# Linear attention into four experts: chunk loads ahead of w2, scaling ahead of the state update, late first updates, casts tied to stages

## The chip, the core and the metric

The kernel runs on one core of a Trainium2 chip. The core has five engines, each with its own instruction queue that it works off in order: TensorE (PE; its weight loads are shown apart as PEld), VectorE (DVE), ScalarE (ACT), GpSimd (POOL) and SyncE (SP), which here issues nearly all transfers. They wait for one another by semaphores. The metric is the device time of one execution in microseconds, lower is better.

## The reference

Two parts, one after the other, all in fp32:

```python
# attention, per batch b (4) and head h (8), head_dim 48, over t = 0..767
cur   = outer(u * k[t], v[t])
y[t]  = r[t] @ (state + cur)
state = w[:, None] * state + outer(k[t], v[t])
# experts: x is y as 3072 rows x 384; 4 experts, D = 384, F = 1024
p    = domain_probs / (domain_probs.sum(-1) + 1e-9)
out += p[:, e] * (relu(x @ w1[e]) @ w2[e])      # for each e
```

## The kernel before

**Tiling.** The 768 time steps of a batch are cut into 6 chunks of 128. Chunk number `ci` counts over batches first (`b = ci % 4`, `c = ci // 4`), so chunks 0 to 3 are the first 128 steps of all four batches and make one sub-sequence of 512 rows for the experts; there are 6 sub-sequences and 24 chunks. Weights are loaded as fp32 in three pieces per expert and matrix (`load_w1`, `load_w2`) into 8 staging buffers `wst`, and rounded to bf16 by `cast_w1`, `cast_w2` on ScalarE ("A") or VectorE ("V"). A piece can be loaded only when the cast eight pieces earlier has freed its buffer.

**One chunk of attention** goes through these steps. `load` brings r, k, v (192 KB each, four buffers of each). `scale_rk` multiplies r and k by powers of w on VectorE (lines 214, 215) into `RK`, of which there are four. `ruk_vb` multiplies r, k and u on GpSimd and rounds v. `stRK` transposes RK on TensorE (line 246) and copies the result out on ScalarE (254); for chunks 8 and up it is a transposing transfer. `diag` sums r·u·k on VectorE (230) and multiplies it with v on GpSimd (231, `dv`). `stAt` makes the 128 x 128 score blocks on TensorE (261) and masks them on VectorE (267). `stY` multiplies with the old state (278) and with v (285), and VectorE adds dv and rounds (289, `Ysb`). `stX` transposes Ysb (328) and VectorE copies it (329) to `xTe`, the experts' input. `stS` makes the state update on TensorE (306), then VectorE (315 in the first chunk of a batch, else 317) and GpSimd (318).

**Experts.** `l1` makes one 128-wide slice of the hidden layer for 512 rows (three matmuls, line 341; ScalarE's Relu, 345), `l1q` four slices for one chunk (355, 359), `l2` one chunk's output (eight matmuls, 368), weighted on ScalarE for expert 0 (374) and added up on VectorE for the others (376).

**PSUM.** Score blocks, transposes and the pair Y and state update have one buffer each (tags `At`, `tr`, `ys`); the expert outputs share four (`mm`). A step that writes into one of the single buffers waits until the last reader of the step before is done.

**Order.** All queues follow the order in which the program calls the helpers. A hand-written list (lines 389 to 454) holds chunks 0 to 3, with expert 0 of sub-sequence 0 woven in; `spin` puts matmuls of no use between, and only keeps TensorE at work. After it a loop goes over slots, one for each expert and sub-sequence: 12 places per slot, eight `l1` of this expert and four `l2` of the slot before. Attention steps of chunks 4 and up come from `att_steps()`, three for every four places in the first three slots, then one for every two. The table `casts` ties casts and loads to places of the slots; from chunk 4 on `diag` also loads the next chunk not yet loaded, starting with chunk 8.

Of the kernel before, what the change touches and what calls it, by code (L numbers as in the profile page):

```python
# [18 lines left out]
def kernel(  # L19
# [367 lines left out]
    with tc.manual_schedule(engines={ET.PE, ET.Pool, ET.DVE, ET.Activation, ET.SP}):  # L387

        wu_consts()
# [56 lines left out]
        stX(3)
        stS(3)
        for i in range(3):
            cast_w1(1, i, "AVA"[i])
# [3 lines left out]
        l1q(0, 0, 0, 3)
        l1q(0, 0, 4, 3)


        casts = {(0, 1): [lambda: cast_w2(1, 0, "A")], (0, 2): [lambda: cast_w2(1, 1, "V")],
                 (0, 6): [lambda: cast_w2(1, 2, "A"), lambda: (load_w2(2), load(6))],
                 (0, 7): [lambda: cast_w1(2, 0, "A")], (0, 8): [lambda: cast_w1(2, 1, "V")],
                 (0, 10): [lambda: cast_w1(2, 2, "A"), lambda: (load_w1(3), load(7))],  # L460
                 (1, 2): [lambda: cast_w2(2, 0, "A")], (1, 3): [lambda: cast_w2(2, 1, "V")],
                 (1, 5): [lambda: cast_w2(2, 2, "A"), lambda: load_w2(3)],
                 (1, 9): [lambda: cast_w1(3, 0, "A")], (1, 10): [lambda: cast_w1(3, 1, "V")],
                 (1, 11): [lambda: cast_w1(3, 2, "A")],
                 (2, 7): [lambda: cast_w2(3, 0, "A")], (2, 8): [lambda: cast_w2(3, 1, "V")],
                 (2, 9): [lambda: cast_w2(3, 2, "A")]}

        def att_steps():

            for ci in range(SUB, 2 * SUB):  # L470
# [4 lines left out]
                if ci == 2 * SUB - 1:
                    yield lambda: (head(2 * SUB), diag(2 * SUB))
                yield lambda ci=ci: stX(ci)
                yield lambda ci=ci: stS(ci)
# [71 lines left out]
```

## Time and profile before

| | us |
|---|---|
| median of 3 runs (316.89 to 319.53) | 319.11 |
| profiled execution | 318.16 |
| its span, first to last instruction | 316.4 |
| TensorE busy | 294.4 (93%) |
| VectorE, ScalarE, GpSimd busy | 162.7, 154.7, 106.0 |

The mean granted clock of TensorE is 0.987. The busy time of TensorE is its matmuls' own time; how it is spread over the span, and what it waited for where it was idle, is read from stretches and from the timeline. Idle time of another engine matters only where TensorE waits for what that engine makes.

### The profile page before, as it was taken

How to read it: one execution, taken by the hardware profiler on the slowest of the kernel's cores; microseconds unless marked ns; L12 is line 12 of the kernel's file. 1: busy time of each engine (PE TensorE's matmuls, PEld its weight loads, DVE VectorE, ACT ScalarE, POOL GpSimd, SP SyncE). 2: the span in 40 equal slices, each digit the busy share in tenths (PEclk: the TensorE clock that was granted, in tenths of full speed). 3: DMA queues.
4: the chain of work that ended last, by engine and by line, in shares of the span. 5: the costliest groups of instructions: out<-in, count | busy, mean ns of one | idle time of the engine just before them, and what ended most of it. 6: DMA issues, size and time to landing. Idle time of an engine off the chain costs nothing.

```text
span 316.4 us, 5360 instructions
## 1 busy us (share of the span) xinstructions
PE 294.4 (93%) x2048; PEld 161.1 (51%) x2081; DVE 162.7 (51%) x292; ACT 154.7 (49%) x249; POOL 106.0 (34%) x137
## 2 busy tenths in 40 slices
PE   6896987878999999999999999999999999999995
PEld 3355643434545555555555555555555555555552
DVE  5785867574954556754464673475461432201223
ACT  4555696634435644345534446434446344465440
POOL 3543335535642542552462364165441000000000
PEclk9997999997999999999999999999999999999999
DMA  8989999999577626446515645810432000200002
GB/s 188 244 247 299 253 269 277 275 225 229 108 172 170 79 43 123 77 117 147 108 33 102 133 102 121 110 33 16 96 85 46 15 12 0 77 25 0 2 0 99
DMA packets 111053, 37.63 MB, mean 119 GB/s; under 512 B 99226, under 2 KB 111004, under 8 KB 111028
## 3 DMA queue, kind: packets, MB, share of 16 engines
q1 hardware_dynamic: 111012, 37.29, 51.0%
q8 instruction: 16, 0.26, 0.4%
q14 instruction: 9, 0.07, 0.1%
q10 hardware_dynamic: 16, 0.00, 0.0%
HBM read 26.79 MB, written 4.72 MB: 100 GB/s over the span
## 4 chain that ended last, share of the span: by engine, by line
PE 80%; DVE 11%; ACT 3%; POOL 2%; issue 2%; DVEq 0%; POOLq 0%
PE out_ps L368 37%; PE hT_ps L341 34%; DVE AtM L267 3%; PE At_ps L261 2%; DVE RK L215 2%; PE Y_ps L285 2%; DVE RK L214 1%; ACT w_sb L84 1%; DVE oacc L376 1%; DVE Ysb L289 1%; PE spin_ps L164 1%; DVE dcoef L230 1%; PE Y_ps L278 1%; ACT hTs L345 1%; PE hT_ps L355 1%
## 5 line engine op out<-in xcount | busy, mean ns | idle before, releaser
L345 ACT ACTIVATE hTs<-hT_ps 128x512 bf16<-128x512 f32 x184 | 109.8, 598 | 114.6 <-PE hT_ps L341 106.8
L368 PE MATMUL out_ps<-w_sb,hTs 128*128 128x384 bf16 x768 | 141.2, 328 | 0.0
L341 PE MATMUL hT_ps<-xTe,w_sb 128*128 128x512 bf16 x519 | 138.1, 380 | 1.9 <-issue 0.2
L368 PEld LDWEIGHTS <-hTs 128*128 128x128 bf16 x768 | 75.1, 98 | 58.5 <-issue 1.7
L376 DVE SCALAR_TENSOR_TENSOR oacc<-out_ps,p_nat,oacc 128x384 f32<-128x384 f32 x72 | 44.3, 615 | 96.1 <-PE out_ps L368 92.0
L341 PEld LDWEIGHTS <-w_sb 128*128 128x128 bf16 x552 | 50.0, 98 | 46.0
L318 POOL TENSOR_TENSOR S<-Tn,wC 64x192 bf16<-64x192 f32 x32 | 17.1, 534 | 89.3 <-DVE Tn L317 82.3
L267 DVE TENSOR_TENSOR AtM<-At_ps,mask 128x512 bf16<-128x512 f32 x48 | 30.9, 685 | 17.0 <-PE At_ps L261 17.0
L222 POOL TENSOR_TENSOR ruk<-Rt,Kt 128x384 f32<-128x384 f32 x24 | 25.5, 1061 | 12.7 <-DMA Kt<-in_k_dram 11.4
L231 POOL TENSOR_TENSOR dv<-Vt,dcoef 128x384 f32<-128x384 f32 x24 | 20.4, 848 | 27.1 <-DVE dcoef L230 27.1
L223 POOL TENSOR_TENSOR ruk<-ruk,U_sd 128x384 f32<-128x384 f32 x24 | 27.1, 1130 | 2.8 <-ACT U_sd L177 1.0
L215 DVE TENSOR_TENSOR RK<-Kt,W_sd 128x384 bf16<-128x384 f32 x24 | 25.9, 1081 | 0.0
L374 ACT ACTIVATE oacc<-out_ps,p_nat 128x384 f32<-128x384 f32 x24 | 14.0, 583 | 17.6 <-PE out_ps L368 17.6
L230 DVE TENSOR_REDUCE dcoef<-ruk 128x8 f32<-128x384 f32 x24 | 13.1, 544 | 9.9 <-POOL ruk L223 9.8
L84 ACT CAST w_sb<-wst 128x1152 bf16<-128x1152 f32 (+1 forms) x18 | 17.7, 1008 | 0.0
L289 DVE TENSOR_TENSOR Ysb<-Y_ps,dv 128x384 bf16<-128x384 f32 x24 | 13.2, 552 | 8.2 <-PE Y_ps L285 6.8
L214 DVE TENSOR_TENSOR RK<-Rt,W_sd 128x384 bf16<-128x384 f32 x24 | 16.3, 677 | 2.2 <-ACT W_sd L175 2.1
L317 DVE TENSOR_TENSOR Tn<-S,St_ps 64x192 f32<-64x192 bf16 x32 | 11.3, 352 | 11.8 <-PE St_ps L306 10.8
L224 POOL CAST Vb<-Vt 128x384 bf16<-128x384 f32 x24 | 16.3, 681 | 0.0
L285 PE MATMUL Y_ps<-Vb,AtM 128*128 128x48 bf16 x192 | 10.0, 184 | 3.7 <-DVE AtM L267 2.4
L246 PE MATMUL RKT_ps<-ident,RK 128*128 128x128 bf16 x64 | 6.1, 232 | 7.8 <-DVE RK L214 3.6
L254 ACT COPY RKT<-RKT_ps 128x1024 bf16<-128x1024 bf16 x7 | 7.1, 1012 | 9.0 <-PE RKT_ps L246 9.0
(55 smaller groups left out, 113.5 us busy)
## 6 DMA issues: line engine op xcount, KB each, us to landing
wst<-in_moe_w_dram SPq DMA_DIRECT2D x16, 576.0 KB, 6.0
Rt<-in_r_dram SPq DMA_DIRECT2D x24, 192.0 KB, 3.4
Kt<-in_k_dram SPq DMA_DIRECT2D x24, 192.0 KB, 3.7
Vt<-in_v_dram SPq DMA_DIRECT2D x24, 192.0 KB, 5.3
out_dram<-oacc SPq DMA_DIRECT2D x24, 192.0 KB, 2.7
wst<-in_moe_w_dram SPq DMA_DIRECT2D x8, 384.0 KB, 6.8
RKT<-RK SPq DMA_TRANSPOSE x16, 3.2
xTe<-Ysb SPq DMA_TRANSPOSE x16, 2.5
```

The source lines that it names most:

```text
L84: nc.scalar.copy(o, i)
L214: nc.vector.tensor_mul(RK[:, 0, :, 0:D], Rt, W1_sd)
L215: nc.vector.tensor_mul(RK[:, 1, :, 0:D], Kt, W2_sd)
L222: nc.gpsimd.tensor_mul(ruk, s["Rt"], s["Kt"])
L223: nc.gpsimd.tensor_mul(ruk, ruk, U_sd)
L231: nc.gpsimd.tensor_mul(dv, s["Vt"], dcoef.to_broadcast((128, H, D)))
L267: nc.vector.tensor_mul(s["AtM"][:, j], ps[:, j], mask[:, None, :].to_broadcast((128, NP, C)))
L318: nc.gpsimd.tensor_mul(S_new[pr, :, cl], Tn[pr], wCb)
L341: nc.tensor.matmul(ps[:, 0:n, :].rearrange("p a b -> p (a b)"), w1_sb[:, e, db, fb * 128:(fb + 1) * 128], xTe[:, db, s0:s0 + n, :].rearran ...
L345: nc.scalar.activation(hTs[:, fb, s0:s0 + n, :], ps[:, 0:n, :], AF.Relu)
L368: nc.tensor.matmul(ps, hTs[:, fb, s, :], w2_sb[:, e, fb, :], start=(fb == 0), stop=(fb == NFB - 1))
L376: nc.vector.scalar_tensor_tensor(oaccs[ci], in0=ps, scalar=pe, in1=oaccs[ci], op0=ALU.mult, op1=ALU.add)
```

## The change

Six things, in the order of the diff. The spin matmuls read a tile of ones of their own, written first of all on VectorE, and there are 29 instead of 24, three of them at the very start. Chunks 2 and 3 are loaded ahead of expert 0's w2. The bank in which p is transposed is one of the four shared ones. `diag` of chunk 4 loads nothing any more, so chunk 8 is loaded by chunk 5's. In the hand-written list `diag` and `scale_rk` stand earlier, casts of w2 are spread, and the state updates of chunks 0 to 3 move behind it: chunk 0's to its end, the other three into the first slot. In the slots `scale_rk` of the next chunk stands between a chunk's `stY` and `stX`, and casts are keyed by attention step instead of by place.

```diff
+    spin_in = consts.tile([128, 4, 128], BF16)
+    nc.vector.memset(spin_in, 1.0)
...
     load(1)
-    load(2)
     prow = consts.tile([TOTC, C, E], F32)
     nc.sync.dma_start(prow, moe_domain_probs.rearrange("(n p) e -> n p e", p=C))
+    load(2)
+    load(3)
     load_w2(0)
-    load(3)
...
-            nc.tensor.matmul(ps, ident, mask[:, None, :].to_broadcast((128, 4, 128)),
-                             start=True, stop=True)
+            nc.tensor.matmul(ps, spin_in[:, 0, :], spin_in, start=True, stop=True)
...
-        pp = psum.tile([128, E, TOTC], F32, tag="ys", bufs=1, name="p_ps")
+        pp = psum.tile([128, E, TOTC], F32, tag="mm", bufs=4, name="p_ps")
...
-        if ci >= SUB and loaded[0] < TOTC:
+        if ci > SUB and loaded[0] < TOTC:
...
         scale_rk(1)
         ruk_vb(1)
-        stS(0)
         spin(2)
         l1q(0, 0, 0, 0)
         stRK(1)
+        diag(1)
         scale_rk(2)
-        diag(1)
         ruk_vb(2)
         l1q(0, 0, 4, 0)
         spin(2)
         stAt(1)
         stRK(2)
+        diag(2)
         spin(4)
         stY(1)
-        spin(3)
+        load_w1(1)
+        spin(2)
         stX(1)
         stAt(2)
-        stS(1)
-        diag(2)
+        scale_rk(3)
+        ruk_vb(3)
+        load(4)
         l1q(0, 0, 0, 1)
         l1q(0, 0, 4, 1)
-        for i in range(3):
-            cast_w2(0, i, "A")
-        load_w1(1)
-        load_w2(1)
-        load(4)
         stY(2)
-        scale_rk(3)
-        ruk_vb(3)
+        stRK(3)
+        cast_w2(0, 0, "A")
+        diag(3)
         spin(2)
         stX(2)
-        stRK(3)
+        stAt(3)
+        l1q(0, 0, 0, 2)
+        cast_w2(0, 1, "A")
+        load_w2(1)
+        load(5)
         p_consts()
...
+        casts = {("At", 4): [c2(1, 0)], ("Y", 4): [c2(1, 1)],
+                 ("H", 4): [c2(1, 2), lambda: (load_w2(2), load(6))],
+                 ("X", 4): [c1(2, 0)], ("S", 4): [c1(2, 1)],
+                 ("At", 5): [c1(2, 2), lambda: (load_w1(3), load(7))],
+                 ("H", 5): [c2(2, 0)], ("X", 5): [c2(2, 1)],
+                 ("S", 5): [c2(2, 2), lambda: load_w2(3)],
+                 ("At", 6): [c1(3, 0)], ("Y", 6): [c1(3, 1)], ("H", 6): [c1(3, 2)],
+                 ("Y", 7): [c2(3, 0)], ("H", 7): [c2(3, 1)], ("X", 7): [c2(3, 2)]}
...
+            yield lambda: (scale_rk(SUB), ruk_vb(SUB))
             for ci in range(SUB, 2 * SUB):
-                yield lambda ci=ci: (scale_rk(ci), ruk_vb(ci))
-                yield lambda ci=ci: (stRK(ci), diag(ci))
-                yield lambda ci=ci: stAt(ci)
-                yield lambda ci=ci: stY(ci)
...
+                yield step("RK", ci, lambda: stRK(ci), lambda: diag(ci))
+                yield step("At", ci, lambda: stAt(ci))
+                yield step("Y", ci, lambda: stY(ci))
+                if ci + 1 < 2 * SUB:
+                    yield step("H", ci, lambda: scale_rk(ci + 1), lambda: ruk_vb(ci + 1))
+                else:
+                    yield step("H", ci, lambda: head(ci + 1), lambda: diag(ci + 1))
+                yield step("X", ci, lambda: stX(ci))
+                yield step("S", ci, lambda: stS(ci))
...
+        late = {(0, 1): [lambda: stS(1)], (0, 5): [lambda: stS(2)], (0, 9): [lambda: stS(3)]}
```

In the order the change shows itself as follows; each row is an instruction of one engine's queue. First VectorE in the hand-written list, from the masking of chunk 2 on, before (RK_135 and RK_137 are chunk 3's):

```order
L267 TENSOR_TENSOR AtM<-At_ps,mask 128x512 x2
L315 TENSOR_TENSOR S_1_143<-St_ps,wC 64x4x48 x2
L230 TENSOR_REDUCE dcoef<-ruk 128x8
L289 TENSOR_TENSOR Ysb<-Y_ps,dv 128x384
L214 TENSOR_TENSOR RK_135<-Rt,W_sd 128x8x48
L215 TENSOR_TENSOR RK_135<-Kt,W_sd 128x8x48
L329 COPY xTe<-xT_ps 128x3x128
```

and with the change:

```order
L268 TENSOR_TENSOR AtM<-At_ps,mask 128x512 x2
L215 TENSOR_TENSOR RK_137<-Rt,W_sd 128x8x48
L216 TENSOR_TENSOR RK_137<-Kt,W_sd 128x8x48
L290 TENSOR_TENSOR Ysb<-Y_ps,dv 128x384
L231 TENSOR_REDUCE dcoef<-ruk 128x8
L330 COPY xTe<-xT_ps 128x3x128
L268 TENSOR_TENSOR AtM<-At_ps,mask 128x512 x2
```

The scaling of chunk 3 stands ahead of the rounding of chunk 2's Y, and the state update of chunk 1 is gone from between.

Then SyncE's queue around chunk 6, before (the three Rt are of chunks 5, 8 and 6, the three wst the pieces of expert 2's w2):

```order
L107 DMA Rt_600<-in_r_dram 128x8x48
L107 DMA Kt_601<-in_k_dram 128x8x48
L107 DMA Vt_602<-in_v_dram 128x8x48
L107 DMA Rt_696<-in_r_dram 128x8x48
L107 DMA Kt_697<-in_k_dram 128x8x48
L107 DMA Vt_698<-in_v_dram 128x8x48
L79 DMA wst_720<-in_moe_w2_dram 128x3x384
L79 DMA wst_722<-in_moe_w2_dram 128x3x384
L79 DMA wst_724<-in_moe_w2_dram 128x2x384
L107 DMA Rt_726<-in_r_dram 128x8x48
L107 DMA Kt_727<-in_k_dram 128x8x48
L107 DMA Vt_728<-in_v_dram 128x8x48
```

and with the change (pieces of expert 2's w1 and w2, then chunks 6 and 8):

```order
L73 DMA wst_606<-in_moe_w1_dram 128x3x384
L73 DMA wst_608<-in_moe_w1_dram 128x3x384
L73 DMA wst_610<-in_moe_w1_dram 128x3x256
L79 DMA wst_748<-in_moe_w2_dram 128x3x384
L79 DMA wst_750<-in_moe_w2_dram 128x3x384
L79 DMA wst_752<-in_moe_w2_dram 128x2x384
L107 DMA Rt_754<-in_r_dram 128x8x48
L107 DMA Kt_755<-in_k_dram 128x8x48
L107 DMA Vt_756<-in_v_dram 128x8x48
L107 DMA Rt_811<-in_r_dram 128x8x48
L107 DMA Kt_812<-in_k_dram 128x8x48
L107 DMA Vt_813<-in_v_dram 128x8x48
```

Chunk 8 now follows chunk 6, and expert 2's w1 and w2 stand together behind chunk 5.

Last VectorE around the scaling of chunk 7 (RK3), before:

```order
L86 CAST w1_sb_70<-wst_783 128x3x384
L289 TENSOR_TENSOR Ysb_1003<-Y_ps_990,dv_947 128x384
L376 SCALAR_TENSOR_TENSOR oacc_667<-out_ps_1006,p_nat_166,oacc_667 128x384
L329 COPY xTe_762<-xT_ps_1016 128x3x128
L317 TENSOR_TENSOR Tn_1037<-S2_1_145,St_ps_1032 64x192 x2
L376 SCALAR_TENSOR_TENSOR oacc_554<-out_ps_1042,p_nat_166,oacc_554 128x384
L214 TENSOR_TENSOR RK3_135<-Rt_787,W1_sd_162 128x8x48
L215 TENSOR_TENSOR RK3_135<-Kt_788,W2_sd_163 128x8x48
L230 TENSOR_REDUCE dcoef_1075<-ruk_1054 128x8
```

and with the change:

```order
L290 TENSOR_TENSOR Ysb_1006<-Y_ps_993,dv_951 128x384
L86 CAST w1_sb_70<-wst_843 128x3x384
L377 SCALAR_TENSOR_TENSOR oacc_659<-out_ps_1009,p_nat_168,oacc_659 128x384
L215 TENSOR_TENSOR RK3_137<-Rt_847,W1_sd_164 128x8x48
L216 TENSOR_TENSOR RK3_137<-Kt_848,W2_sd_165 128x8x48
L330 COPY xTe_777<-xT_ps_1038 128x3x128
L377 SCALAR_TENSOR_TENSOR oacc_564<-out_ps_1043,p_nat_168,oacc_564 128x384
L318 TENSOR_TENSOR Tn_1058<-S2_1_147,St_ps_1053 64x192 x2
L231 TENSOR_REDUCE dcoef_1079<-ruk_1021 128x8
```

The scaling has moved ahead of the copy of chunk 6's transposed Y, of one multiply-add and of chunk 6's state update.

## Rows read from the trace of the kernel before

**Rows 1.** Stretches: start:end length, busy per engine, PEclk, DMA share, GB/s.

```profile
0.00:38.20 38.20, 30.03 (x277) 18.62 (x279) 25.54 (x60) 19.97 (x29) 15.30 (x26) 0.96 0.94 246
38.20:50.10 11.90, 8.98 (x72) 4.65 (x73) 8.72 (x13) 9.94 (x16) 5.65 (x7) 1.00 0.99 253
50.10:66.10 16.00, 14.09 (x116) 7.41 (x116) 10.63 (x19) 10.09 (x14) 7.58 (x10) 1.00 1.00 267
66.10:83.00 16.90, 14.24 (x96) 7.46 (x97) 10.74 (x20) 7.54 (x11) 9.03 (x12) 0.90 0.87 203
...
88.00:316.40 228.40, 223.25 (x1463) 121.03 (x1489) 102.32 (x176) 105.94 (x178) 64.20 (x80) 1.00 0.35 74
```

**Rows 2.** Timeline, TensorE: start, us, instruction, [idle before, releaser].

```profile
24.78 0.34 PE L328 MATMUL xT_ps<-ident,Ysb 128*128 128x128 bf16 x3 [1.28 <-DVE Ysb L289]
...
26.78 0.61 PE L246 MATMUL RKT_ps<-ident,RK 128*128 128x128 bf16 x8 [1.66 <-DVE xTe L329]
...
38.21 1.24 PE L341 MATMUL hT_ps<-xTe,w_sb 128*128 128x512 bf16 x5
...
49.15 0.40 PE L246 MATMUL RKT_ps<-ident,RK 128*128 128x128 bf16 x4 [1.56 <-DVE RK L214]
```

**Rows 3.** Timeline from w1's cast to the next sub-sequence.

```profile
61.26 1.16 ACT L84 CAST w_sb<-wst 128x1152 bf16<-128x1152 f32 x1
...
65.91 0.62 DVE L376 SCALAR_TENSOR_TENSOR oacc<-out_ps,p_nat,oacc 128x384 f32<-128x384 f32 x1
...
66.44 0.35 DVE L329 COPY xTe<-xT_ps 128x384 bf16<-128x384 bf16 x1
...
69.62 1.16 DVE L214 TENSOR_TENSOR RK<-Rt,W_sd 128x384 bf16<-128x384 f32 x1
...
70.70 1.34 DVE L215 TENSOR_TENSOR RK<-Kt,W_sd 128x384 bf16<-128x384 f32 x1
...
70.84 0.40 PE L246 MATMUL RKT_ps<-ident,RK 128*128 128x128 bf16 x4 [1.14 <-DVE RK L214]
...
72.11 0.40 PE L246 MATMUL RKT_ps<-ident,RK 128*128 128x128 bf16 x4 [0.87 <-DVE RK L215]
...
83.03 0.81 PE L341 MATMUL hT_ps<-xTe,w_sb 128*128 128x512 bf16 x3
```

**Rows 4.** SyncE's transfers: issue time in ns, start, landing; chunks 7, 6, w1.

```profile
L107 SPq DMA_DIRECT2D Rt<-in_r_dram x1: 679/679/679, 56.6 to 56.6; - x1
DMA to landing us min/median/max: 7.3/7.3/7.3
...
L107 SPq DMA_DIRECT2D Kt<-in_k_dram x1: 1032/1032/1032, 50.0 to 50.0; - x1
DMA to landing us min/median/max: 6.3/6.3/6.3
...
L73 SPq DMA_DIRECT2D wst<-in_moe_w_dram x1: 591/591/591, 54.9 to 54.9; - x1
DMA to landing us min/median/max: 5.7/5.7/5.7
```

**Rows 5.** Timeline, VectorE, a scaling without GpSimd beside it.

```profile
78.89 0.55 DVE L214 TENSOR_TENSOR RK<-Rt,W_sd 128x384 bf16<-128x384 f32 x1
...
79.36 0.55 DVE L215 TENSOR_TENSOR RK<-Kt,W_sd 128x384 bf16<-128x384 f32 x1
```

**Rows 6.** Waits of SyncE: us in total, times, longest.

```profile
SPq L107 <- POOL dv L231: 9.4, 6, 3.0
```

**Rows 7.** Chain of waits, one L1 and one L2 group.

```profile
78.31 0.65 PE hT_ps L341 x3
78.96 1.30 PE out_ps L368 x8
```

**Rows 8.** Stretches, the two with a low clock (PEclk behind POOL).

```profile
26.80:30.40 3.60, 3.60 (x36) 3.28 (x35) 1.00 (x4) 1.61 (x2) 0.96 (x2) 0.69 1.02 359
72.30:76.10 3.80, 3.58 (x16) 1.54 (x16) 0.21 (x1) 1.61 (x2) 3.34 (x5) 0.55 1.06 224
```

More of the change, by code (lines that the diff above doesn't have):

```diff
@@ L387 @@
     with tc.manual_schedule(engines={ET.PE, ET.Pool, ET.DVE, ET.Activation, ET.SP}):
+        spin(3)
         wu_consts()
@@ L395 @@
         w_consts()
-        spin(3)
+        spin(1)
         stAt(0)
@@ L399 @@
             cast_w1(0, i, "A")
-        spin(3)
+        spin(4)
         stY(0)
@@ L416 @@
         stRK(2)
+        diag(2)
         spin(4)
         stY(1)
-        spin(3)
+        load_w1(1)
+        spin(2)
         stX(1)
         stAt(2)
-        stS(1)
-        diag(2)
+        scale_rk(3)
+        ruk_vb(3)
+        load(4)
         l1q(0, 0, 0, 1)
         l1q(0, 0, 4, 1)
-        for i in range(3):
-            cast_w2(0, i, "A")
-        load_w1(1)
-        load_w2(1)
-        load(4)
         stY(2)
-        scale_rk(3)
-        ruk_vb(3)
+        stRK(3)
+        cast_w2(0, 0, "A")
@@ L434 @@
+        diag(3)
         spin(2)
         stX(2)
-        stRK(3)
+        stAt(3)
[3 more added lines that the diff above has]
+        load(5)
         p_consts()
-        l1q(0, 0, 0, 2)
         l1q(0, 0, 4, 2)
-        stAt(3)
-        diag(3)
-        stS(2)
+        stY(3)
+        cast_w2(0, 2, "A")
+        spin(3)
+        stX(3)
+        spin(1)
+        cast_w1(1, 0, "A")
+        cast_w1(1, 1, "V")
         l2(0, 0, 0)
-        stY(3)
+        l1q(0, 0, 0, 3)
@@ L445 @@
         l2(0, 0, 1)
[L446 to L449, printed above, removed]
+        l1q(0, 0, 4, 3)
+        cast_w1(1, 2, "A")
         load_w1(2)
-        load(5)
         l2(0, 0, 2)
[L453 to L466, printed above, removed]
+        stS(0)
@@ new lines, in c1, with c2 @@
+        def c1(e, i):
+            return lambda: cast_w1(e, i, "AVA"[i])
+        def c2(e, i):
+            return lambda: cast_w2(e, i, "AVA"[i])
+        casts = {("At", 4): [c2(1, 0)], ("Y", 4): [c2(1, 1)],
[6 more added lines that the diff above has]
+                 ("Y", 7): [c2(3, 0)], ("H", 7): [c2(3, 1)], ("X", 7): [c2(3, 2)]}
@@ L468, in att_steps, with step, do @@
+        def step(name, ci, *fs):
+            def do():
+                for f in fs:
+                    f()
+                for f in casts.get((name, ci), ()):
+                    f()
+            return do
         def att_steps():
+            yield lambda: (scale_rk(SUB), ruk_vb(SUB))
             for ci in range(SUB, 2 * SUB):
-                yield lambda ci=ci: (scale_rk(ci), ruk_vb(ci))
-                yield lambda ci=ci: (stRK(ci), diag(ci))
-                yield lambda ci=ci: stAt(ci)
@@ L474, in att_steps @@
-                yield lambda ci=ci: stY(ci)
[L475 to L478, printed above, removed]
+                yield step("RK", ci, lambda: stRK(ci), lambda: diag(ci))
[5 more added lines that the diff above has]
+                    yield step("H", ci, lambda: head(ci + 1), lambda: diag(ci + 1))
@@ L503 @@
                 for g in range(3):
-                    for f in casts.get((si, 3 * q + g), ()):
+                    for f in late.get((si, 3 * q + g), ()):
                         f()
```

## The prediction

> **What bounds the kernel now.** I read the stretches first, then the waits inside them. After 88 us TensorE is busy 223.25 of 228.40 us [rows 1], so nothing that the change does can come from there; what it does before 88 us is either kept to the end or lost. The first four stretches are the prologue (to 38.2) and the slots of experts 1, 2 and 3 on sub-sequence 0 (to 50.1, 66.1 and 83.0). TensorE idles in them 8.2, 2.9, 1.9 and 2.7 us by subtraction. In the same rows the transfers are the second bound: the DMA share is 0.94 to 1.00 up to 66.1 us, at 246 to 267 GB/s. So before 66 us the work can be made earlier only as far as its bytes have landed.
>
> The waits themselves: TensorE waits for VectorE. In the prologue 1.28 us for Y's rounding of chunk 2 and 1.66 us for the copy that frees the one transpose bank [rows 2]; in the expert-1 slot 1.56 us for the scaling of chunk 5 [rows 2]; at chunk 7 1.14 and 0.87 us for its two scalings [rows 3]. In rows 3 the reader is to see why the last is late: VectorE is done with its multiply-add at 65.91 + 0.62 = 66.53, then come the transposed copy and the state update, and only at 69.62 the scaling of chunk 7, whose r had landed at 56.6 + 7.3 = 63.9 us [rows 4]. The transfer was 5.7 us early, and the order of the program was what held it.
>
> **The change, part by part.**
>
> *Scaling ahead of the state update.* For chunk 7 it now stands right behind the multiply-add, ahead of the copy and of the state update. Two bounds. If nothing upstream moves, it starts at 66.53 and saves 69.62 − 66.53 = 3.1 us. If upstream moves by 2.6 us or more, it waits for r at 63.9 and saves 5.7 us; it can't save more, since chunk 7's transfer stands behind the same bytes as before (chunks 0 to 6 and 8, three pieces each of w1 of experts 0 to 3 and of w2 of experts 0 to 2, in either order). I take the second, 63.95, since the next parts move more than 2.6 us.
>
> What the move costs there: both engines that read r and k are now released by the same landing, so GpSimd multiplies beside the scaling. Alone the two instructions take 0.55 us each [rows 5]; beside GpSimd they took 1.16 and 1.34 us [rows 3]. I take the slow pair: 63.95 + 2.50 = 66.45. The transposed copy of chunk 6 (0.35 us, rows 3) is now behind it on VectorE and frees the transpose bank, so the eight transposes, half of which used to run during the scaling, all start at 66.45 + 0.35 + 0.14 of hand-offs (two gaps of 0.07, as between 70.70 + 1.34 = 72.04, the scaling's end, and the transposes at 72.11) = 66.9 and take 0.61 (the eight of [rows 2]), to 67.5. Before, they ended at 72.11 + 0.40 = 72.5. **Saved: 5.0 us.** [...]
>
> *Does upstream move by 2.6 us?* In the prologue chunk 3 (3 x 192 KB) no longer stands behind w2 of expert 0 (576 + 576 + 384 KB), which at 246 GB/s was 6.4 us of transfer; r, k of chunk 3 are scaled ahead of Y's rounding of chunk 2, so their transposes come in the place of the wait of 1.66 us; dv is ready a stage earlier because diag follows stRK, which takes the wait of 1.28 us. Together 2.9 us, against 38.21 for the first expert-1 matmul [rows 2]. In the expert-1 slot the wait of 1.56 us for chunk 5 goes the same way. That is 4.5 us of named waits, of which 2.6 are needed; the 1.9 over are not a gain, they are cover. Out of this cover I pay what I cost at nothing: the memset of the spin operand, 29 spin matmuls in place of 24, the casts now tied to stages, and w2 of expert 0, which lands one chunk (590 KB / 246 GB/s = 2.4 us) later. If the cover is gone, each us too late costs one us until only 3.1 are saved.
>
> *Loads.* Chunk 8 was loaded in chunk 4's diag, ahead of chunk 6; now chunk 5's diag does it, behind chunk 6. Chunk 6's k had landed at 50.0 + 6.3 = 56.3 [rows 4]; without chunk 8 ahead of it, 2.2 to 2.4 us earlier (590 KB at 267 and 246 GB/s), about 54.0. It is needed when chunk 5's Y has been rounded, some 51 to 52 by the same shift, so VectorE waits there up to 2.5 us: that is where most of the prologue's gain ends, and why I don't count it. The loads by diag waited 9.4 us in all on SyncE for dv of the same chunk [rows 6]; now their buffers are a stage older, so this wait goes, but SyncE's wait cost TensorE nothing.
>
> w1 of expert 3: first piece at 54.9 + 5.7 = 60.6 [rows 4], the same bytes ahead of it as before. Its cast takes 1.16 us [rows 3], so expert 3's slot can start at 61.8 instead of 66.1 [rows 1]. From there to the transposes of chunk 7 at 66.9 it has three L1 groups (0.65 each) and one L2 group (1.30) [rows 7], 3.3 us, and a few small transposes: TensorE waits there about 1.5 us, and this transfer sets nothing.
>
> *The four late state updates* are 16 small matmuls and 8 VectorE instructions, the same as before, in other places; they share one PSUM bank with Y, and I put a wait of 0.5 us each on TensorE for it, all ahead of 50 us and so under the cover.
>
> *Behind chunk 7.* [...] The one behind chunk 7 costs 3.8 x (1 − 0.55) = 1.7 us, and I take it as gone: one wait of about 1.5 us is left there in place of 1.14 and 0.87 with matmuls between. **Saved: 1.7.** [...]
>
> VectorE's backlog at 67 us (copy, multiply-add, state update, reduction: about 2.5 us) makes chunk 7's masking late by about **0.5 us, lost**. From expert 3's slot on the order is as before, TensorE-bound at 98% [rows 1], and the gain is kept.
>
> Sum: 5.0 + 1.7 − 0.5 = 6.2 us off the profiled execution's 318.16 us (span 316.4): **312.0 us**. The median of the three runs is 319.11 and the profiled execution lies 0.95 below it, inside their spread of 316.89 to 319.53; I keep 312.0 and let the range carry the 0.95.
>
> **The rivals.**
>
> *The clock falls once more* at the wait behind chunk 7 or chunk 6. For: two such falls in the trace. Against: single waits, as the 1.56 us in rows 2, left the clock at 1.00 in rows 1. Price 1.7 us: 313.7.
>
> *The wait moves, and the gain with it.* VectorE and ScalarE take their work in order, and the change puts instructions that need a transfer (scaling of chunks 6 and 7, casts of w1 of expert 3) ahead of evictions that need none. If the transfers come 2.6 us or more behind those of before, because SyncE meets a buffer that a later cast frees, chunk 7 is scaled at 66.5 as in the lower bound: 3.1 + 0 − 0.5 = 2.6 saved with the clock's fall kept, 315.6; 4 us behind, 317. For: DMA share 1.00, no slack in the stream. Against: equal bytes ahead, and SyncE's waits were for dv, which now go.
>
> [...]
>
> **How the numbers follow.** Forecast at full clock 0.42, one fall of the clock 0.28, the moved wait 0.20, the long low clock 0.10. A measurement of this kernel can tell about 1% (3.2 us) from no change; the first two cases are beyond that (0.70 faster), the third within it (0.20), the last slower (0.10). Likeliest time 312.0. Range: down to 308.5, if the scaling of chunk 7 takes its lone 1.1 us instead of 2.5 and its transfer comes 1 us sooner, with the 1.2 us by which the lowest run stands under the profiled one; up to 317, which takes in the fall and nearly all of the moved wait. The long low clock and the end of the third case are left out.
>
> **What would show it.** Right: the first scaling of chunk 7 at 64 us, ended by a DMA; its transposes done by 68; expert 3's slot from about 62 and the first matmul of the next sub-sequence (83.03 before, rows 3) at 76 to 77; granted clock 1.00 there; the rest as long as before. Wrong: chunk 7's r later than 65 us, VectorE idle for a transfer over 3 us, or a clock under 0.9 in a slot.

## The result and the profile after

The changed kernel takes 310.12 us (median of 4, 309.42 to 311.79) against 319.32 us (316.89 to 320.03) beside it on the same chip: a ratio of 0.9733, 95% interval [0.9668, 0.9797]. In two later comparisons it took 309.78 us, 0.9767 [0.9724, 0.9809], and 309.95 us, 0.9732 [0.9692, 0.9773]. One execution of the changed kernel (313.75 us) and one of the kernel before (320.19 us) lie over 1.5% above the fastest of their kernel and count as slow; the medians 309.95 here and 318.0 below include them (309.34 and 317.8 without), and no argument below rests on them. Forecast were 312.0 us and a range of 308.5 to 317.0. The first profiled execution took 311.79 us, the longest of the four, with a span of 310.0, 6.4 us under the span of before.

The stretches of the changed kernel, cut as in [rows 1] and [rows 8] (length, then busy us and instruction count of PE, PEld, DVE, ACT and POOL, PEclk, DMA share, GB/s):

```profile
0.00:38.20 38.20, 31.83 (x279) 18.97 (x284) 24.11 (x57) 21.95 (x32) 18.01 (x28) 1.00 0.95 253
38.20:50.10 11.90, 10.62 (x96) 5.87 (x96) 9.64 (x19) 10.36 (x16) 4.70 (x7) 1.00 1.04 303
50.10:66.10 16.00, 15.47 (x128) 9.18 (x130) 13.13 (x25) 10.58 (x17) 8.06 (x10) 1.00 0.97 237
66.10:83.00 16.90, 13.77 (x100) 7.32 (x101) 12.02 (x21) 6.31 (x11) 10.66 (x14) 0.90 1.04 217
...
88.00:310.00 222.00, 216.98 (x1425) 117.65 (x1449) 99.44 (x170) 103.46 (x174) 62.22 (x77) 1.00 0.34 73
...
26.80:30.40 3.60, 3.37 (x42) 2.58 (x44) 2.82 (x8) 2.96 (x5) 0.00 (x0) 1.00 0.98 245
72.30:76.10 3.80, 2.45 (x16) 1.20 (x15) 3.62 (x8) 1.97 (x4) 3.18 (x4) 1.00 1.07 205
76.50:80.80 4.30, 3.40 (x21) 1.77 (x22) 1.75 (x3) 0.60 (x1) 2.12 (x3) 0.75 1.09 207
```

From 88 us to the end TensorE idles 5.0 us, as before (5.2): what is left to do there has become 6.3 us less, so the gain was made before 88 us, as the first reading said it had to be. TensorE's idle time in the first three stretches fell from 8.2, 2.9 and 1.9 us to 6.4, 1.3 and 0.5. In the fourth it did not fall: 2.7 before, 3.1 after. Both stretches with a low clock of [rows 8] are at 1.00, and a new one at 0.75 stands from 76.5 to 80.8.

TensorE's timeline of the same execution shows why (start, us, instruction, count, idle time before and its releaser). The lines answer to [rows 2] and to the TensorE rows of [rows 3]:

```profile
23.80 0.40 PE L247 MATMUL RKT_ps<-ident,RK 128*128 128x128 bf16 x4 [0.41 <-DVE RK L215]
...
26.13 0.33 PE L329 MATMUL xT_ps<-ident,Ysb 128*128 128x128 bf16 x3 [0.72 <-ACT RKT L255]
...
35.83 0.81 PE L342 MATMUL hT_ps<-xTe,w_sb 128*128 128x512 bf16 x2
...
60.91 1.46 PE L342 MATMUL hT_ps<-xTe,w_sb 128*128 128x512 bf16 x6
...
64.48 0.61 PE L247 MATMUL RKT_ps<-ident,RK 128*128 128x128 bf16 x8
...
73.94 0.81 PE L342 MATMUL hT_ps<-xTe,w_sb 128*128 128x512 bf16 x3
77.40 0.40 PE L262 MATMUL At_ps<-RKT 64*128 64x128 bf16 x8 [2.65 <-DMA RKT<-RK]
78.39 2.49 PE L369 MATMUL out_ps<-w_sb,hTs 128*128 128x384 bf16 x8
...
80.99 0.52 PE L286 MATMUL Y_ps<-Vb,AtM 128*128 128x48 bf16 x8
```

In the prologue the waits of 1.28 and 1.66 us are down to 0.72 and 0.41, and the first expert-1 matmul comes at 35.83 instead of 38.21 [rows 2]; the slot of expert 3 starts at 60.91. The eight transposes of chunk 7 run without a wait and end at 64.48 + 0.61 = 65.09 instead of 72.5, and the first matmul of the next sub-sequence starts at 73.94 instead of 83.03 [rows 3], 9.1 us earlier. Of these 9.1 a new wait takes back 2.65: the mask product of chunk 8 waits for chunk 8's transposing transfer. Behind it the eight matmuls of one output take 2.49 us, where elsewhere in the trace they take 1.46. One thing is gained on the way: chunk 8's matmuls with v start at 80.99 without a wait, where the kernel before had one of 0.92 us for their masking:

```profile
87.31 0.27 PE L285 MATMUL Y_ps<-Vb,AtM 128*128 128x48 bf16 x4 [0.92 <-DVE AtM L267]
```

VectorE, GpSimd and SyncE in the same timeline, around chunks 6, 7 and 8 (SPq is SyncE's issuing):

```profile
52.83 0.56 DVE L216 TENSOR_TENSOR RK<-Kt,W_sd 128x384 bf16<-128x384 f32 x1 [0.20 <-DMA Kt<-in_k_dram]
...
55.46 0.67 SPq L107 DMA_DIRECT2D Rt<-in_r_dram  x1
...
62.78 0.56 DVE L215 TENSOR_TENSOR RK<-Rt,W_sd 128x384 bf16<-128x384 f32 x1
63.32 0.56 DVE L216 TENSOR_TENSOR RK<-Kt,W_sd 128x384 bf16<-128x384 f32 x1
63.43 1.31 POOL L223 TENSOR_TENSOR ruk<-Rt,Kt 128x384 f32<-128x384 f32 x1 [5.16 <-DMA Kt<-in_k_dram]
...
66.76 4.14 SPq L107 DMA_DIRECT2D Vt<-in_v_dram  x1
...
70.58 0.85 DVE L216 TENSOR_TENSOR RK<-Kt,W_sd 128x384 bf16<-128x384 f32 x1
...
73.74 1.53 SPq L241 DMA_TRANSPOSE RKT<-RK  x1
```

Chunk 6's k was there at 52.8, not at 54.0. The load of chunk 7's r is issued at 55.46 (56.6 before [rows 4]). Chunk 7 is scaled from 62.78, without a wait for a transfer, and its two instructions take 0.56 us each: GpSimd, which also waits for k, starts 0.11 us behind the second one, and it is GpSimd's multiply that is long (1.31). Chunk 8 is scaled by 70.58 + 0.85 = 71.43, but SyncE is still issuing: chunk 9's v for 4.14 us, then chunk 10's three loads. The transfer is issued at 73.74, and TensorE has it at 77.40.

### The profile page after: what moved, and what is told of

Read it like the earlier page. It is cut to its first block, busy times and chain, and to the rows that moved or that the text cites. A ratio compares the mean times of both kernels' runs of the same rounds, so it can differ in the third digit from the quotient of the medians.

```text
span 310.0 us, 5368 instructions
## 1 busy us (share of the span) xinstructions
PE 293.7 (95%) x2050; PEld 161.8 (52%) x2086; DVE 160.4 (52%) x293; ACT 154.7 (50%) x249; POOL 105.7 (34%) x137
## 4 chain that ended last, share of the span: by engine, by line
PE 85%; DVE 5%; DMA 3%; POOL 2%; SPq 2%; issue 1%; ACT 0%; DVEq 0%; POOLq 0%; ACTq 0%
PE out_ps L369 41%; PE hT_ps L342 37%; DMA Kt<-in_k_dram 2%; PE At_ps L262 2%; DVE AtM L268 2%; PE Y_ps L286 1%; DMA RKT<-RK 1%; PE St_ps L307 1%; PE Y_ps L279 1%; SPq L107 1%; PE RKT_ps L247 1%; POOL ruk L223 1%; POOL ruk L224 1%; PE hT_ps L356 1%; DVE S L316 1%
## 5 line engine op out<-in xcount | busy, mean ns | idle before, releaser
L216 DVE TENSOR_TENSOR RK<-Kt,W_sd 128x384 bf16<-128x384 f32 x24 | 24.2, 1009 | 0.2 <-DMA Kt<-in_k_dram 0.2
L215 DVE TENSOR_TENSOR RK<-Rt,W_sd 128x384 bf16<-128x384 f32 x24 | 14.2, 593 | 2.4 <-ACT W_sd L176 2.1
L262 PE MATMUL At_ps<-RKT 64*128 64x128 bf16 x192 | 9.7, 222 | 3.4 <-DMA RKT<-RK 2.6
L166 PE MATMUL spin_ps<-spin_in 128*128 128x512 bf16 x26 | 10.8, 514 | 1.6 <-DVE spin_in L112 1.5
L262 PEld LDWEIGHTS <-RKT 64*128 64x128 bf16 x192 | 5.6, 95 | 12.5 <-issue 6.6
```

Source lines behind the costliest of these rows:

```text
L216: nc.vector.tensor_mul(RK[:, 1, :, 0:D], Kt, W2_sd)
L262: nc.tensor.matmul(ps[:, j, q, :], s["RKT"][j * P2:(j + 1) * P2, 1, q, :], s["RKT"][j * P2:(j + 1) * P2, 0, q, :], start=True, stop=True)
```

## The experiments

Three theories were to be told apart: T, that the place of the scaling (with GpSimd's multiplies of the same step, which move with it) ahead of the state update carries the gain; P, that the prologue does; L, that the order of the loads does.

**The scaling put back (first form).** The step H goes behind X and S again:

```diff
-                if ci + 1 < 2 * SUB:
-                    yield step("H", ci, lambda: scale_rk(ci + 1), lambda: ruk_vb(ci + 1))
-                else:
-                    yield step("H", ci, lambda: head(ci + 1), lambda: diag(ci + 1))
                 yield step("X", ci, lambda: stX(ci))
                 yield step("S", ci, lambda: stS(ci))
+                if ci + 1 < 2 * SUB:
+                    yield step("H", ci, lambda: scale_rk(ci + 1), lambda: ruk_vb(ci + 1))
+                else:
+                    yield step("H", ci, lambda: head(ci + 1), lambda: diag(ci + 1))
```

> The changed kernel with one thing undone: in the slots the scaling of the next chunk (and the head of chunk 8) stands behind the state update again. Theory T (the gain comes from the place of the scaling, which was bound by program order and is now bound by its transfer): chunk 7's transposes come 2 to 4 us later than 64.5; part of it is hidden, since the changed kernel waits 2.65 us for chunk 8's transposing transfer anyway; 312 to 315 us. Rival P (the gain is the prologue's, carried through) and rival L (it is the loads', chunk 6 ahead of chunk 8): 310 to 311 us, no change against the changed kernel.

Measured 324.48 us, ratio 1.019 [1.0163, 1.0217]: slower than the kernel before, which no theory expected. The edit did too much: chunk 8's preparation (`head(8)`) and the casts that are tied to H moved along. Its timeline (SyncE, then TensorE):

```profile
85.12 1.33 SPq L241 DMA_TRANSPOSE RKT<-RK  x1
...
88.39 0.40 PE L262 MATMUL At_ps<-RKT 64*128 64x128 bf16 x8 [2.90 <-DMA RKT<-RK]
92.72 0.27 PE L286 MATMUL Y_ps<-Vb,AtM 128*128 128x48 bf16 x4 [1.70 <-DVE AtM L268]
```

The transfer of chunk 8 is issued at 85.12, and two waits follow, of 2.90 and 1.70 us, where the kernel before has none and one of 0.92. This run decides nothing between T, P and L. Beside the next run (316.0 us) it shows that moving chunk 8's preparation and those casts along costs some 8 us; which of the two does is not shown.

**The scaling put back (chunks 5 to 7 alone).** Chunk 8's preparation and all casts keep their places:

```diff
-                    yield step("H", ci, lambda: scale_rk(ci + 1), lambda: ruk_vb(ci + 1))
+                    yield step("H", ci)
...
-                yield step("S", ci, lambda: stS(ci))
+                if ci + 1 < 2 * SUB:
+                    yield step("S", ci, lambda: stS(ci), lambda: scale_rk(ci + 1),
+                               lambda: ruk_vb(ci + 1))
+                else:
+                    yield step("S", ci, lambda: stS(ci))
```

> The changed kernel with the scaling of chunks 5, 6 and 7 alone put back behind the state update of the chunk before; chunk 8's preparation and the weights' casts keep their places, which an earlier kernel had moved too. Theory T (the scaling's place ahead of the state update carries the gain): chunk 7's transposes end at 71 to 73 us instead of 65.1, the first matmul of the next sub-sequence comes at 79 to 82 us instead of 73.9, and the time is 315 to 319. Rival H (the early place of chunk 8's preparation carries it, and the scaling's place is hidden by the steps that follow): transposes late, but the next sub-sequence at 74 to 76 and the time 310 to 313.

Measured 316.0 us, ratio 0.9932 [0.9906, 0.9959] to before; the changed kernel in the same comparison 309.78. Its timeline, VectorE and TensorE:

```profile
70.51 0.86 DVE L216 TENSOR_TENSOR RK<-Kt,W_sd 128x384 bf16<-128x384 f32 x1
70.64 0.40 PE L247 MATMUL RKT_ps<-ident,RK 128*128 128x128 bf16 x4 [1.14 <-DVE RK L215]
71.43 0.40 PE L247 MATMUL RKT_ps<-ident,RK 128*128 128x128 bf16 x4 [0.39 <-DVE RK L216]
...
80.78 0.81 PE L342 MATMUL hT_ps<-xTe,w_sb 128*128 128x512 bf16 x3
81.52 0.40 PE L262 MATMUL At_ps<-RKT 64*128 64x128 bf16 x8
```

T holds in all three numbers: transposes done at 71.43 + 0.40 = 71.8, next sub-sequence at 80.78, 316.0 us. The wait of 1.14 us of [rows 3] is back with everything else of the change in place. And chunk 8 has no wait here: it appears where chunk 7 is early (2.65 us above, 1.71 in the next experiment).

**The scaling alone**, in the kernel before, with nothing else of the change:

```diff
-            for ci in range(SUB, 2 * SUB):
-                yield lambda ci=ci: (scale_rk(ci), ruk_vb(ci))
+            yield lambda: (scale_rk(SUB), ruk_vb(SUB))
+            for ci in range(SUB, 2 * SUB):
...
                     yield lambda: (head(2 * SUB), diag(2 * SUB))
+                else:
+                    yield lambda ci=ci: (scale_rk(ci + 1), ruk_vb(ci + 1))
```

> The kernel before with this one thing done: in the slots the scaling of the next chunk stands between Y and the transposes of the chunk before, ahead of the state update; list, loads and places of casts as before. Theory T: the lower bound of the prediction, chunk 7 scaled at 66.5 or somewhat sooner (64 to 66.5) instead of 69.6, 314 to 317 us. Rivals P and L: 318 to 320 us, since neither the list nor the loads are touched.

Measured 312.25 us, 0.9817 [0.9786, 0.9849], better than T expected; P and L fall as what carries the gain. Chunk 7 in its timeline (GpSimd, VectorE, TensorE):

```profile
64.27 1.00 POOL L222 TENSOR_TENSOR ruk<-Rt,Kt 128x384 f32<-128x384 f32 x1 [3.10 <-DMA Kt<-in_k_dram]
64.69 0.99 DVE L214 TENSOR_TENSOR RK<-Rt,W_sd 128x384 bf16<-128x384 f32 x1
65.61 1.35 DVE L215 TENSOR_TENSOR RK<-Kt,W_sd 128x384 bf16<-128x384 f32 x1
...
67.47 0.61 PE L246 MATMUL RKT_ps<-ident,RK 128*128 128x128 bf16 x8
```

Here GpSimd is first, and the two scalings take 2.34 us in place of 1.12. The transposes end at 68.1, near the 67.5 of the prediction: with the loads and the prologue of before, the prediction's picture of chunk 7 is right nearly as drawn.

**The loads alone** in the kernel before (chunks 2 and 3 ahead of w2, the later loads moved as in the change):

```diff
-    load(2)
...
+    load(2)
+    load(3)
     load_w2(0)
-    load(3)
...
-        if ci >= SUB and loaded[0] < TOTC:
+        if ci > SUB and loaded[0] < TOTC:
```

> The kernel before with the loads alone moved: chunks 2 and 3 ahead of expert 0's w2, chunk 4 ahead of expert 1's w2, chunk 5 ahead of expert 2's w1, and no load by chunk 4's diag, so that chunk 8 comes behind chunk 6. Theory T: the scalings of chunks 5, 6 and 7 stand behind the state updates and were not waiting for their transfers, so 317 to 320 us. Rival L: 312 to 316 us. Rival P, as far as the prologue waited for chunk 3: 316 to 318 us.

Measured 318.60 us, 1.0015 [0.9981, 1.0049]: no difference. L falls.

**The old prologue, run twice.** The hand-written list and the first loads of before, and from the expert-1 slot on all of the change but the late state updates:

```diff
-    load(2)
-    load(3)
     load_w2(0)
+    load(3)
...
-        late = {(0, 1): [lambda: stS(1)], (0, 5): [lambda: stS(2)], (0, 9): [lambda: stS(3)]}
+        late = {}
```

> The changed kernel's slots and its loads by diag behind the hand-written list and the first loads of before (state updates of chunks 0 to 3 in the list, none late; spins on the new tile). Theory T: the prologue's 2.5 us are cover; VectorE then waits less for chunks 6 and 7 and the time is 310 to 312 us. Rival P: the prologue's gain is lost one for one and more, 313 to 318 us.

> The new slots from expert 1 on behind the old hand-written list and the old first loads, a second time, beside the changed kernel. Theory T of the prediction (the prologue's gain is absorbed by the waits for chunks 6 and 7, which depend on transfers): within 1 us of the changed kernel, and the transposes of chunk 7 within 1 us of 65.1. Rival P (the prologue's gain arrives in part): slower than the changed kernel by 1.2 us or more, and the first matmul of the next sub-sequence later than 73.9 by as much.

Measured 311.32 us, 0.9796 [0.9748, 0.9844], and 311.23 us, 0.9771 [0.9737, 0.9805], beside which the changed kernel took 309.95. The intervals overlap with the changed kernel's, but the median lies 1.3 us above the one beside it, the first 1.2 to 1.5 above those of other comparisons, and the traces say the same. From the second one, a stretch and TensorE's timeline:

```profile
28.00:32.00 4.00, 4.00 (x41) 3.44 (x41) 1.56 (x5) 1.99 (x3) 0.07 (x1) 0.57 1.05 373
```

```profile
67.29 0.61 PE L247 MATMUL RKT_ps<-ident,RK 128*128 128x128 bf16 x8
...
76.75 0.81 PE L342 MATMUL hT_ps<-xTe,w_sb 128*128 128x512 bf16 x3
78.42 0.40 PE L262 MATMUL At_ps<-RKT 64*128 64x128 bf16 x8 [0.86 <-DMA RKT<-RK]
```

Chunk 7's transposes end at 67.9, 2.8 us behind the changed kernel's: the new prologue's gain does arrive at chunk 7. What it is worth in the end is less, since chunk 8 waits only 0.86 us there. From the first one, the same stretch, then SyncE, VectorE and TensorE:

```profile
28.00:32.00 4.00, 3.10 (x45) 2.12 (x43) 3.03 (x8) 1.88 (x4) 1.22 (x3) 1.00 1.01 360
...
58.26 1.04 SPq L107 DMA_DIRECT2D Rt<-in_r_dram  x1
...
65.27 0.56 DVE L215 TENSOR_TENSOR RK<-Rt,W_sd 128x384 bf16<-128x384 f32 x1 [0.23 <-DMA Rt<-in_r_dram]
66.11 0.56 DVE L216 TENSOR_TENSOR RK<-Kt,W_sd 128x384 bf16<-128x384 f32 x1 [0.28 <-DMA Kt<-in_k_dram]
...
79.72 0.61 PE L262 MATMUL At_ps<-RKT 64*128 64x128 bf16 x8 [2.46 <-DMA RKT<-RK]
```

This execution, 314.06 us, had no low clock in the prologue: its first expert-1 matmul came at 36.55, the other's at 38.58. Still chunk 7's transposes ended at 66.99 + 0.61 = 67.6, for its r and k landed late. The clock fell later instead, to 0.56 from 80.0 to 83.6, behind the wait of 2.46 us. So the same order starts expert 1 up to 2.0 us apart, some 1.3 of it behind 27 us, where the one execution had its low clock; what arrives at chunk 7 hangs on the transfers. The second form of theory T (transposes within 1 us of 65.1) falls; P's 1.2 us is met, just. In all ten executions of this kernel the granted clock of the whole was 0.989 to 0.994, in ten of fifteen of the changed kernel 0.998 or more; the two profiles show that the low clock of the old prologue's kernel has no fixed place.

**The new wait: the transfer's place.** Chunk 10's loads go behind chunk 8's transposing transfer. The changed kernel ran beside it once more as the mark:

```diff
-        if ci > SUB and loaded[0] < TOTC:
-            load(loaded[0])
-            loaded[0] += 1
+        for _ in range(0 if ci == 2 * SUB - 1 else 2 if ci == 2 * SUB else 1):
+            if ci > SUB and loaded[0] < TOTC:
+                load(loaded[0])
+                loaded[0] += 1
```

> The changed kernel once more, as the mark for the three kernels beside it. Expected of every theory: 309 to 312 us. The wait ahead of the mask product of chunk 8 (its first matmul at about 77 us) is there again, 2.0 to 2.7 us, and the granted clock in the five microseconds behind it may or may not fall below 0.95: in the runs so far the clock of the whole execution lay between 0.994 and 1.000.

> The changed kernel with chunk 10's three loads issued behind the transposing transfer of chunk 8 instead of ahead of it (with chunk 11's, at the next chunk's preparation). Theory Q (the 2.65 us wait ahead of chunk 8's mask product is the transfer's place behind three load issues on SyncE's queue): the transfer is issued at 71.5 instead of 73.7, its wait falls to 0.5 us or less, and the time falls by 1.5 to 3 us against the changed kernel in the same comparison, to 307 to 308.5. Rival D (the transfer would be no earlier, because the issue of chunk 9's v blocks SyncE until the data engines are free, or because the transfer's landing is held up by other transfers): issued at or after 73, wait 2 us or more, time 309.5 to 311. Rival M (the wait goes, and the mask product's wait for something else, or the next chunk's transfer, takes its place): wait gone there, time 309.5 to 311.

Measured 309.32 us, 0.9736 [0.9706, 0.9767], beside 309.78: no difference that can be told. The mark's profile, an execution with a span of 307.7 us at a clock of 1.00, says why (SyncE and TensorE):

```profile
72.13 1.81 SPq L241 DMA_TRANSPOSE RKT<-RK  x1
...
76.15 0.40 PE L262 MATMUL At_ps<-RKT 64*128 64x128 bf16 x8 [1.36 <-DMA RKT<-RK]
```

The same program issued the transfer 1.6 us earlier than in the first profile (chunk 9's v held SyncE for 3.52 us, there for 4.14), and the wait was 1.36 us, with no fall of the clock behind it. With the loads behind the transfer:

```profile
72.68 1.44 SPq L242 DMA_TRANSPOSE RKT<-RK  x1
...
76.26 0.40 PE L263 MATMUL At_ps<-RKT 64*128 64x128 bf16 x8 [0.60 <-DMA RKT<-RK]
...
79.74 0.27 PE L287 MATMUL Y_ps<-Vb,AtM 128*128 128x48 bf16 x4 [0.86 <-DVE AtM L269]
```

Q falls as a source of time. In this profile, of the longest of its five executions (310.53 us), chunk 8 was scaled at 71.77 + 0.85 = 72.62 and the transfer went out at once, so the queue was no longer in the way; but with chunk 10's loads behind it, too, 3.6 us (76.26 − 72.68) lie between issue and use. The wait that is left, 0.60, is followed by one of 0.86 for the masking, as rival M had it.

**The new wait filled with matmuls.**

```diff
-                yield lambda ci=ci: stAt(ci)
+                if ci == 2 * SUB:
+                    yield lambda ci=ci: (spin(12), stAt(ci))
+                else:
+                    yield lambda ci=ci: stAt(ci)
```

> The changed kernel with 12 matmuls on constant data (2.6 us of TensorE time) put ahead of chunk 8's mask product, to fill the wait. Theory C (the fall of the clock after that wait costs the time, the wait itself stands in any case): granted clock 1.00 from 76 to 81 us in the profile, and the time falls by 0.7 to 1.5 us against the changed kernel, the spread between runs shrinks. Rival N (the fall comes from something else, or costs nothing): clock below 0.95 there again, or time equal within 0.5 us. Against both: if the wait is not there in this kernel, the filling costs up to 2.6 us and the time rises.

Measured 310.53 us, 0.9768 [0.9736, 0.9799], beside 309.78. The filling took 2.75 us ahead of the mask product, which started at 76.98 without a wait, 0.8 us later than the mark's, and the clock was 1.00 from 76.5 to 80.8. The gain that C expected is not there: where the wait is 1.4 us, the filling costs nearly what a fall of the clock would (1.1 us in the first profile), and in two of its six executions the clock was at 0.994 all the same.

**Chunk 8 transposed on TensorE** in place of the transfer:

```diff
-        if ci >= 2 * SUB:
+        if ci > 2 * SUB:
             s["RKT"] = work.tile([128, 2, NP, C], BF16, tag="RKT", bufs=3, name="RKT")
```

> The changed kernel as the mark for the two kernels beside it: 309 to 311 us by every theory, with a wait of 1.3 to 2.7 us ahead of chunk 8's mask product.

> The changed kernel with chunk 8's scaled r and k transposed by TensorE and copied by ScalarE instead of by a transfer of SyncE. Theory W (the transfer's whole way, 3.6 to 4.0 us from its issue to the mask product wherever it stands in the queue, is what chunk 8 waits for): the wait of 1.4 to 2.7 us is gone, eight transposes of 0.61 us in all and possibly a wait of up to 0.7 us for the scaling come in, so the time falls by 0.5 to 1.5 us against the changed kernel beside it, to 308.3 to 309.5. Rival M (another wait takes its place: the scaled k comes late, or the mask product then waits for ScalarE's copy): waits of 1.4 us or more at the transposes or at the mask product, time equal within 0.5 us. Rival X (the transposes share one PSUM tile with the transposes of Ysb and hold them up): slower by 0.5 us or more.

Measured 311.81 us, 0.9801 [0.9766, 0.9837], beside 309.95. In its timeline:

```profile
71.28 0.86 PE L247 MATMUL RKT_ps<-ident,RK 128*128 128x128 bf16 x8 [0.55 <-DVE RK L215]
...
76.95 0.40 PE L262 MATMUL At_ps<-RKT 64*128 64x128 bf16 x8
...
80.50 0.27 PE L286 MATMUL Y_ps<-Vb,AtM 128*128 128x48 bf16 x4 [0.92 <-DVE AtM L268]
```

The transfer's wait is gone, as W said, but the scaling's wait of 0.55 and the transposes take its place, and the masking is waited for 0.92 us, where the mark's execution has no wait. Against that execution chunk 7's transposes start 0.8 us later (65.34 against 64.52), chunk 8's mask product still 0.8 (76.95 against 76.15), and the masked blocks are used 1.8 later (80.50 against 78.72): about 1.0 of the 1.9 us by which it is slower comes from the edit's waits, and 0.8 was there before chunk 8. Rival X's number is met, not its mechanism: the transposes wait for the scaling, not for their tile. These 0.8 go with a lower clock (0.994 to 0.998 in all six executions; in the profiled one 0.77 to 0.81 from 24 to 32 us, in the prologue, where the order of instructions is that of the changed kernel). Why the edit should bring that stays open.

**Chunk 8 prepared one stage earlier**, with the loads behind its transfer as above:

```diff
-                yield step("At", ci, lambda: stAt(ci))
+                if ci + 1 < 2 * SUB:
+                    yield step("At", ci, lambda: stAt(ci))
+                else:
+                    yield step("At", ci, lambda: stAt(ci), lambda: head(ci + 1))
...
-                    yield step("H", ci, lambda: head(ci + 1), lambda: diag(ci + 1))
+                    yield step("H", ci, lambda: diag(ci + 1))
```

> The changed kernel with chunk 8's scaling and transposing transfer moved forward, from behind chunk 7's Y to right behind chunk 7's mask product, and chunk 10's loads put behind that transfer. Theory W (what chunk 8 waits for is a transfer of 3.6 to 4.0 us that starts too late): chunk 8 is scaled by 70 us instead of 71.4 to 71.6, the transfer is issued right behind the last load of chunk 9 at about 70 to 71 instead of 72.1 to 75.4, no wait over 0.3 us ahead of chunk 8's mask product, and the granted clock keeps 1.00 from 76 to 84 us. The median then falls by 0.5 to 1.5 us below the changed kernel's 309.8 to 310.1, to 308.3 to 309.4, with fewer executions above 311. Rival V (VectorE does chunk 8's scaling ahead of chunk 7's Y, and what it delays there costs as much as the wait): chunk 7's Y or its rounding later by 1 us or more, time 309.5 to 311.

Measured 309.65 us (308.94 to 310.34), 0.9742 [0.9712, 0.9771], in a comparison without the changed kernel beside it. Its timeline (SyncE, TensorE, VectorE):

```profile
70.70 1.37 SPq L242 DMA_TRANSPOSE RKT<-RK  x1
...
74.52 0.40 PE L263 MATMUL At_ps<-RKT 64*128 64x128 bf16 x8
...
75.81 1.35 DVE L216 TENSOR_TENSOR RK<-Kt,W_sd 128x384 bf16<-128x384 f32 x1
...
78.27 0.27 PE L287 MATMUL Y_ps<-Vb,AtM 128*128 128x48 bf16 x4 [1.14 <-DVE AtM L269]
```

The transfer is issued at 70.70 and the wait for it is gone, as W said. One stage later TensorE waits 1.14 us for the masking of chunk 8, which VectorE reaches only behind chunk 9's scaling. The highest of six executions is 310.34, where the changed kernel had one of 312.93, but the median is not lower by more than the runs scatter. No version tried beats the changed kernel by a difference that can be told.

## Why the prediction was right, and where it was not

**What holds.** The four kernels with and without the two halves of the change make a square:

| median, us | scaling behind the state update | scaling ahead of it |
|---|---|---|
| rest as before | 318.0, 318.3, 318.5 | 312.25 |
| rest as in the change | 316.0 | 309.78 |

The scaling's place, for chunks 5 to 7 together, is worth about 6 us in either row (318.0 − 312.25 = 5.8 in one comparison, 316.0 − 309.78 = 6.2 in another); that is the step that the prediction put first. Compared at the same granted clock of 0.999 to 1.000, the put-back scaling took 314.5 to 314.8 us in four executions and the changed kernel beside it 309.1 to 309.9 in four: some 5 us. At chunk 7 the difference is larger, 71.8 − 65.1 = 6.7 us, and the new wait for chunk 8 takes 1.4 of it back.

**5.0 us at chunk 7: mis-sized, 7.4 measured.** Two terms were off, both named as the lower end of the range. The start was put at 63.95, ended by a transfer, as r landed before; the scaling starts at 62.78, when VectorE is done with its multiply-add, so r was there by then, with the same bytes ahead of it. And the scaling was put beside GpSimd at 2.50 us; it took 63.32 + 0.56 − 62.78 = 1.10. The slow pair exists: with the scaling alone it took 2.27 us (64.69 to 65.61 + 1.35), and there GpSimd had started first, at 64.27. With the lone pair of [rows 5], 2 x 0.55 = 1.10 us, in place of 2.50 the prediction's sum gives 312.0 − 1.4 = 310.6, an estimate; it lies 0.5 from the measured 310.1, mine 1.9, but it too knows nothing of the wait at chunk 8.

**"The 1.9 over are not a gain, they are cover": wrong.** The step said that chunk 7 is bound by its landing, which the rest of the change doesn't move, so that what the prologue gains beyond 2.6 us ends in a wait for transfers. But the rest is worth 2.0 to 2.5 us in the square's left column (318.0 to 318.5 against 316.0) and as much in its right one (312.25 − 309.78 = 2.5, from two comparisons), and the old prologue with its first loads makes some 1.3 of it. The reason is in part in the landings: in the first profile of the old prologue chunk 7's r was issued at 58.26 and waited for until 65.27, k until 66.11 (in the second VectorE itself came only at 64.94 and waited 0.16 us for k); with the new one r was issued at 55.46, and the scaling ran from 62.78. The order of the first loads and steps moves when SyncE gets to issue, so the transfers, too, came earlier, and TensorE had no wait at chunk 7 where I expected 1.5 us. I had taken equal bytes ahead for an equal landing. How much of the rest is the low clock of the old prologue was not measured apart.

**"From expert 3's slot on the order is as before ... and the gain is kept": wrong.** The order is as before, but with chunk 7 earlier by 7.4 us, the next transfer in line was not earlier by as much. Chunk 8's scaled r and k took 3.66 us (73.74 to 77.40) and, in the mark's execution, 4.02 us (72.13 to 76.15) to come back transposed; before, and with the scaling put back, that time lay under other work. Now 2.65 and 1.36 us of it are seen. The 0.5 us that I had set for late masking of chunk 7 was not lost: the wait in front of Y's second half is 0.32 us, as before (0.33).

**The low clock behind chunk 7: gone there, as forecast, and back elsewhere.** The granted clock is 1.00 from 72.3 to 76.1, where it was 0.55 [rows 8]; the 1.7 us of the forecast are that stretch's 3.8 x 0.45. In the first profile it fell to 0.75 from 76.5 to 80.8 behind the wait of 2.65 us, a price of 4.3 x 0.25 = 1.1 us; in the second, behind 1.36 us, it did not. The rival "the clock falls once more" thus happens in some executions of the same program: ten of fifteen ran at 0.998 or more and took 309.0 to 310.6 us, five at 0.989 to 0.994 and took 310.2 to 312.9; where the clock fell in those five is known for the profiled one alone. Here the fall came behind a wait of 2.65 us for a transfer; before the change the larger one (0.55) came behind a pair of VectorE waits of 1.14 and 0.87 us. What sets such a fall off was not shown.

**Errors that cancelled.** In the first profile 7.4 us came at chunk 7 (5.0 forecast), 1.7 from the low clock behind it (1.7 forecast), 0.9 from the masking wait of chunk 8 that is gone (nothing forecast) and none was lost on chunk 7's masking (0.5 forecast); the wait for chunk 8's transfer took 2.65 and the fall of the clock 1.1 (nothing forecast for either). That sums to 6.25, beside 6.4 measured and 6.2 forecast: the hit on this execution is luck. For the mark's execution, with a wait of 1.36 us and no fall, the same sum gives 8.6, beside a span shorter by 316.4 − 307.7 = 8.7. So the predicted 312.0 is 1.9 to 2.2 us above the medians, and the right bound came with a wrong account of what follows it.

**The other rivals.** The moved wait (SyncE held up by a buffer) did not come: chunk 7 landed earlier. The long low clock, which had a chance of 0.10, did not come: no slot but the one behind chunk 8 is below 1.00.

## What to carry to other kernels

Where an engine works in order, ask of each instruction on it whether the engine behind waits for it, and put the one that is waited for first: here two instructions of half a microsecond each, moved in three chunks ahead of a state update that nobody needs yet, are worth 6 us. Before counting such a gain to the end, go to the next transfer that depends on the same work: it has a length of its own (3.3 to 4.0 us here), and it turned into the next wait (2.65 us in the first profile) when what had lain over it was gone. And "the same bytes ahead" did not fix a landing here: chunk 7's r, issued at 55.46 us, was there by 62.78; issued at 58.26, it was waited for until 65.27.

## What the runs showed of the hardware

- Chunk 7's two scalings of 128 x 384 took 0.56 us each in the first profile of the changed kernel, where GpSimd's multiply began 0.11 us after the second (62.78 and 63.32; GpSimd from 63.43, 1.31 us). With the scaling alone, where GpSimd's multiply had begun first (64.27, 1.00 us), they took 0.99 and 1.35. In these rows it was the one that came second that paid.
- A transposing transfer of 128 x 1024 bf16 (chunk 8's) took 3.6 us from issue to use with chunk 10's three plain loads issued behind it (72.68 to 76.26), and 3.7 and 4.0 us with them issued ahead of it (73.74 to 77.40, 72.13 to 76.15). In the first form of the put-back scaling, where SyncE had issued nothing between 73.34 (72.64 + 0.70) and 85.12 us, it took 3.3 (85.12 to 88.39).
- A plain load of 192 KB, chunk 9's v, held SyncE for 4.14 us at its issue in the first profile (from 66.76; the DMA share was 0.98 from 66.8 to 70.9), and for 5.04 us in the last experiment (from 65.55). The load behind it in the first profile started at 71.00.
- The granted clock differed between six executions of the changed kernel on one chip (median 309.78 us), and so did the time: four at 0.999 to 1.000 took 309.1 to 309.9 us, one at 0.989 took 311.3 and one at 0.994 took 312.9. In six executions each, the kernel without the wait for chunk 8's transfer scattered less (308.94 to 310.34) than the one with it (309.11 to 312.93); that the wait is the reason was not shown, and the kernel with the wait filled (309.71 to 311.77) speaks against it.
